# Two steps' scores in one phase around each output product, in a kernel of two attentions

## The chip, the cores and the metric

The kernel runs on one core of a Trainium2 chip. The metric is the time of one execution on the device in microseconds; a kernel's time is the median over its runs. The profile is taken from one further execution. TensorE (PE, with its weight loads PEld) multiplies, VectorE (DVE) and ScalarE (ACT) read the results from eight accumulation banks of 128 partitions by 512 numbers, GpSimd (POOL) works in the local memory only, and SP issues most transfers.

## What is computed

Two attention layers with 32 heads of 18 columns over 2048 positions, each with its own input, projections and output weights; their outputs stand side by side.

```python
# A: each position looks at 8 positions, 2 apart
logits = einsum("bhsd,bhswd->bhsw", q, kg) * scale      # masked before position 0
o = einsum("bhsw,bhswd->bhsd", softmax(logits), vg)
a = o.reshape(B, S, D) @ A_wo
# B: each position looks at all positions
scores = einsum("bhqd,bhkd->bhqk", q, k) * scale
o = einsum("bhqk,bhkd->bhqd", softmax(scores), v)
b = o.reshape(B, S, D) @ B_wo
return concatenate([a, b], axis=-1)                      # (1, 2048, 1152)
```

All is in 32-bit numbers. A projection or output product is split into high and low parts, so that one product of 128 by 288 is 27 or 30 matrix multiplications ("pieces") of at most 64 rows each.

## The kernel before

After a stage of projections (lines 373 to 725) the kernel runs 512 steps (the loop at line 1165). Heads are taken in 8 groups of 4, queries in 4 blocks of 512, keys in 16 tiles of 128; `g`, `b` and `kt` name a step's group, block and tile. A step has these parts on TensorE, in the order in which the program lists them, which is the order in which the engine takes them:

- Four score multiplications of 56 rows by 512 columns (`score`, line 269), two on each half of the array's rows (`r` is the half); the halves work side by side. ACT turns each result into exponentials `e` (line 276). `e` tiles come from two pools, six and two of them, by a count modulo 8.
- Three banks of maxima (`maximum` and `parts_of_maximum`, line 158): for a later block the scores are computed a first time, and DVE takes the largest of each 256 numbers (line 166), so that the exponentials don't overflow. One of the three banks is made of two quarters, one from each row half; since two row halves must not write one bank at once, an empty instruction on ACT (line 249) stands between them as a link of semaphores (`sync`).
- The values: four multiplications of all 128 rows by 19 columns (`weigh`, line 739), each recorded as two, which add the previous step's exponentials times the values into the bank `po` over 16 steps. The array has to change from row halves to full height and back once a step.

The banks: scores have four in turn, maxima three ("else"), `po` one.

Beside the steps runs an agenda: functions with due steps (`later`, `plan`, `due`), which issue the loads, the POOL and DVE work of the first attention and the closing of a block. Among them are the output products. Those of the first attention (`finished`, `sums_of_a`; 32 halves) and some of the second (`quarter` by way of `half`) are put into the list `inside`, and the next step takes one before its fourth score (line 1180). `beside` (line 1044) then computes the product in two chains, each row half into a bank of its own, piece by piece in turn, and puts two more maxima between them. ACT copies one bank to `y` (line 973), DVE adds the other (line 974). So a step with a product has five banks of maxima, and the next step three.

When a block's last tile is weighed, `finish` copies `po` (line 749 on ACT, line 752 on DVE). When the maxima have all been taken, near the end, two steps' values are done together (`paired`, line 1195), and products wait in the list `waiting`.

Of the kernel before, what the change touches and what calls it, by code (L numbers as in the profile page):

```python
# [23 lines left out]
NT = S // 128  # L24
NB = S // 512
SCALE = DH ** -0.5
# [7 lines left out]
ALL = NG * STEPS  # L34
# [25 lines left out]
def two_attentions(ctx: ExitStack, tc, xa, wa, woa, xb, wb, wob, out):  # L60
# [5 lines left out]
    nc = tc.nc  # L66
# [39 lines left out]
    step = 0  # L106

    def later(n, f):
        agenda[step + n].append(f)
# [5 lines left out]
    def due():  # L115
        for f in agenda.pop(step, []):
            f()
# [96 lines left out]
    given = [0, 0]  # L214
# [44 lines left out]
    e_room = None  # L259
    counted = [-1]  # L260

    def score(g, b, kt, h, kind="scores", between=None):

        assert (g, b) in placed
        qs, ks = sets[g % 3]
        p, r = divmod(h, 2)
        ps = bank(kind)
        at = slice(64 * r, 64 * r + 56)
        nc.tensor.matmul(ps, ks[at, p, 128 * kt : 128 * kt + 128], qs[at, b, p], start=True, stop=True)  # L269
        if between:  # L270
            between()

        counted[0] += 1
        early = counted[0] % 8 < 6
        e = (e_room if early else work).tile([128, 512], F32, name="e", bufs=6 if early else 2)
        nc.scalar.activation(e, ps, AF.Exp, scale=SCALE)  # L276
        return e

    vs = {}

# [92 lines left out]
    every = slice(0, 512)  # L373
# [4 lines left out]
    with (tc.tile_pool(name="x", bufs=1, side="right") as xp,  # L378
# [4 lines left out]
        early = ExitStack()  # L383
# [98 lines left out]
        if True:  # L482
# [9 lines left out]
            chunks = [[(0, 0, 128)], [(0, 128, third - 128), (D, 0, 256 - third)], [(D, 256 - third, 128)]]  # L492
# [24 lines left out]
            for c in range(5):  # L517
                one, other = (load, nc.scalar.dma_start) if c % 2 == 0 else (nc.scalar.dma_start, load)
# [9 lines left out]
            x = [t[0] for t in xs]  # L528
# [69 lines left out]
            for t in range(NT):  # L598
                ps = bank()
# [78 lines left out]
            for k in range(2, 14):  # L678
                n = 46 if k == 2 else 36 + 4 * k
# [14 lines left out]
            for t in order[:4]:  # L694
                ps = bank()
# [18 lines left out]
            for c, b in order:  # L714
                n = min(128, 3 * D - 128 * c)
# [3 lines left out]
            es = []  # L719
# [10 lines left out]
        step = 0  # L730
# [5 lines left out]
    def weigh(*steps):  # L736
        for g, b, kt, es in steps:
            for i in range(4):
                nc.tensor.matmul(po[32 * i : 32 * i + 19], vs[g][:, kt, 19 * i : 19 * i + 19], es[i],  # L739
                                 start=kt == 0, stop=kt == NT - 1)  # L740
        if kt == NT - 1:
            finish(g, b)
# [116 lines left out]
    def local(j):  # L859

        st = {}
# [98 lines left out]
            x.append(last)  # L960

        def finished(h, n):
            inside.append(lambda: sums_of_a(h, n))

        def sums_of_a(h, n):
            his, los = zip(*wo["a"])
            w = his[:4], los[:4], his[4], los[4]
            cols = slice(288 * h, 288 * h + 288)
            if h == 0:
                st["y"] = ys["a", j, n] = work.tile([128, D], F32, name="y", bufs=4)  # L970
            one, two = beside("scores", *(halves(r, 0, w, st["x", n], cols, slice(0, 128), True) for r in range(2)))
            y = st["y"][:, cols]
            nc.scalar.activation(y, two, AF.Copy)
            behind_scores.append(lambda: nc.vector.tensor_add(y, one, y))

# [50 lines left out]
    ys = {}  # L1026
# [13 lines left out]
    inside = []  # L1040
# [3 lines left out]
    def beside(kind, *both):  # L1044

        sums_ = [bank(k)[:, :288] for k in (kind, None)]
        turns = [[(sums_[r], *ab, i == 0, i == len(t) - 1) for i, ab in enumerate(t)] for r, t in enumerate(both)]
        pair = kind and sum(given) + 2 <= NG * NB * PIECES * 2
        if pair:

            for r in range(2):
                turns[r].insert(6 + 4 * r, None)
        for i in range(max(map(len, turns))):
            for r in range(2):
                if i < len(turns[r]):
                    if turns[r][i]:
                        ps, a, b, start, stop = turns[r][i]
                        nc.tensor.matmul(ps, a, b, start=start, stop=stop)  # L1058
                    else:
                        maximum(r)()  # L1060
        if pair:

            rings["else"].append(rings["else"].pop(0))
        return sums_

    def sum_of(y, t, h, chunks, kind=None):

        pos, cols = slice(128 * t, 128 * t + 128), slice(288 * h, 288 * h + 288)
        both = []
        for r in range(2):  # L1070
            both.append([])
            for c, (hi, lo) in enumerate(chunks):
                at = slice(64 * r, min(64 * r + 64, hi.shape[0]))
                whi, wlo = wo["b"][c]
                both[r] += [(a[at, pos], w[at, cols]) for a, w in ((hi, whi), (hi, wlo), (lo, whi))]
        one, two = beside(kind, *both)
        if kind:
            nc.vector.tensor_copy(y, one)
        else:
            nc.scalar.activation(y, one, AF.Copy)  # L1080
        nc.vector.tensor_add(y, two, y)
# [27 lines left out]
    def full(b, new):  # L1109
        def half(t, h):  # L1110
            if total - sum(given) > 4:
                inside.append(lambda: quarter(t, h, "scores"))
            else:
                waiting.append(lambda: quarter(t, h))

        def quarter(t, h, *kind):
            if h == 0:
                ys[t, b] = work.tile([128, D], F32, name="y", bufs=4)
            sum_of(ys[t, b][:, 288 * h : 288 * h + 288], t, h, [*olds[b], new], *kind)
            if h == 1:  # L1120
                later(1, lambda: load(out[512 * b + 128 * t : 512 * b + 128 * t + 128, D:], ys[t, b]))

        return [(4 + 2 * t + h, lambda t=t, h=h: half(t, h)) for t in range(4) for h in range(2)]

# [34 lines left out]

    total = early + rest  # L1160

    paired = False
    due()
    step += 1
    while step < ALL:
        n, kt = divmod(step, NT)
        g, b = divmod(n, NB)
        es = [None] * 4

        whole = total - sum(given) > 1  # L1170
        parts = (bool(begun) or total - sum(given) > 3) and step not in copied

        ps = bank() if inside and whole else None


        ahead = kt == 0 and (n < 6 or n >= 24)
        part = [parts_of_maximum()] if parts and not ahead else []
        for h in (0, 2, 1, 3):

            if inside and h == 3:  # L1180
                inside.pop(0)()
# [52 lines left out]
```

## Time and profile before

| | |
|---|---|
| runs | 1604.53 us median of 3 (1604.03 to 1605.91) |
| profiled execution | span 1603.8 us from its first to its last instruction; what lies around it is not in the trace |
| TensorE clock granted | 0.998 |
| PE busy | 1590.0 us, 99% |
| DVE busy | 1383.7 us, 86% |
| ACT busy | 1217.7 us, 76% |
| POOL busy | 960.1 us, 60% |

PE's ends are modelled and its instructions overlap, so its 99% does not say that nothing could be gained there. The steps fill the time from about 423 us to the end; before that, and in the last 100 us, other limits hold, so the prices of a step are read from the timeline of that stretch. In a row of the timeline stand the start, the length, engine, line, operation, result and inputs; rows that belong together are merged, and x5 says how many there are. A bracket gives how long the engine stood idle before, and what ended it.

### The profile page before, as it was taken

The numbers are of one execution on the slowest core, as the hardware profiler recorded it, in microseconds if no ns is written. First come the engines' busy times: TensorE is split into PE (matmuls) and PEld (weight loads), VectorE is DVE, ScalarE is ACT, GpSimd is POOL, SyncE is SP. The second block draws the span as 40 slices with busy tenths as digits, with TensorE's granted clock in tenths as the row PEclk, the third lists the DMA queues.
The fourth block names the chain that finished last, engine by engine and source line by source line (L and its number), as shares of the span: only waits on it lengthen the run. The fifth ranks groups of instructions, "written<-read, shape, count | busy, mean of one in ns | idle before, by whom it ended". The sixth has DMA issues, their size and how long they took to land.

```text
span 1603.8 us, 35232 instructions
## 1 busy us (share of the span) xinstructions
PE 1590.0 (99%) x13388; PEld 950.3 (59%) x13388; DVE 1383.7 (86%) x2347; ACT 1217.7 (76%) x2438; POOL 960.1 (60%) x792
## 2 busy tenths in 40 slices
PE   9999999999999999999999999999999999999998
PEld 7999888999543444444444444444444444445676
DVE  5299899999999999999999999999999999999512
ACT  6423441221699999999999999999999999898655
POOL 2405742201166995896797897797797797772100
PEclk9999999999999999999999999999999999999999
DMA  8937954522312362254326325422632231144111
GB/s 247 235 125 199 258 173 124 162 92 80 74 37 67 72 143 72 59 133 99 73 76 143 74 78 131 105 78 61 135 100 65 65 96 32 50 163 157 62 39 60
DMA packets 186058, 172.11 MB, mean 107 GB/s; under 512 B 119152, under 2 KB 132976, under 8 KB 184160
## 3 DMA queue, kind: packets, MB, share of 16 engines
q1 hardware_dynamic: 181024, 158.31, 36.1%
q0 software_dynamic: 4032, 10.63, 3.1%
q8 instruction: 105, 1.72, 0.5%
q10 hardware_dynamic: 832, 0.92, 0.2%
q14 instruction: 65, 0.53, 0.1%
HBM read 96.94 MB, written 71.90 MB: 105 GB/s over the span
## 4 chain that ended last, share of the span: by engine, by line
PE 91%; DVE 4%; DMA 2%; ACT 2%; issue 0%; POOL 0%; SPq 0%; POOLq 0%; DVEq 0%; ACTq 0%
PE po L739 29%; PE bank L269 18%; PE bank L158 17%; PE bank L361 15%; PE bank L1058 8%; PE bank L298 5%; DVE mx L166 3%; ACT e L276 1%; DMA dqk<-olo 1%; DMA dqk<-ohi 1%; DMA den<-o 0%; POOL xlo L409 0%; PE bank L513 0%; DVE as L900 0%; ACT lg L909 0%
## 5 line engine op out<-in xcount | busy, mean ns | idle before, releaser
L166 DVE TENSOR_REDUCE mx<-bank 128x2 f32<-128x512 f32 x2048 | 1288.3, 684 | 110.5 <-PE bank L158 82.6
L276 ACT ACTIVATE e<-bank 128x512 f32<-128x512 f32 x2048 | 1049.9, 608 | 46.6 <-PE bank L269 43.3
L158 PE MATMUL bank<-ks,qs 54*128 54x256 f32 (+1 forms) x2530 | 787.7, 378 | 4.2 <-DVE mx L166 2.5
L158 PEld LDWEIGHTS bank<-ks,qs 54*128 54x128 f32 x2530 | 408.8, 184 | 445.7 <-DVE mx L166 397.0
L269 PE MATMUL bank<-qs,ks 56*128 56x512 f32 x2048 | 568.9, 426 | 0.0
L739 PE MATMUL po<-e,v 128*19 128x512 f32 x4096 | 537.7, 599 | 0.0
L269 PEld LDWEIGHTS bank<-qs,ks 56*128 56x128 f32 x2048 | 299.7, 184 | 29.3 <-ACT e L276 25.2
L882 POOL TENSOR_TENSOR pr<-aq,akv 128x1024 f32<-128x1024 f32 x72 | 158.3, 2200 | 15.8 <-DMA akv<-da 13.0
L925 POOL TENSOR_TENSOR pr<-lg,akv 128x1024 f32<-128x1024 f32 x72 | 158.3, 2199 | 0.6
L886 POOL TENSOR_TENSOR pr<-pr 128x1024 f32<-128x1024 f32 x64 | 152.6, 2384 | 5.0
L739 PEld LDWEIGHTS po<-e,v 128*19 128x19 f32 x4096 | 70.5, 97 | 129.1 <-issue 123.6
L689 ACT ACTIVATE ohi<-bank 128x512 f32<-128x512 f32 (+1 forms) x56 | 30.4, 595 | 150.8 <-issue 104.2
L361 PE MATMUL bank<-xhi,ahi 64*128 64x512 f32 (+1 forms) x448 | 114.3, 387 | 0.0
L361 PE MATMUL bank<-xhi,alo 64*128 64x512 f32 (+1 forms) x448 | 109.6, 387 | 0.0
L361 PE MATMUL bank<-xlo,ahi 64*128 64x512 f32 (+1 forms) x448 | 105.8, 388 | 0.1
L926 POOL TENSOR_TENSOR pr<-pr 128x512 f32<-128x512 f32 x72 | 92.4, 1284 | 5.6
L409 POOL TENSOR_TENSOR alo<-raw,ahi 128x512 fp32r<-128x512 f32 (+1 forms) x14 | 17.6, 1255 | 121.4 <-ACT ahi L408 113.2
L501 POOL TENSOR_TENSOR olo<-olo,ohi 128x512 fp32r<-128x512 f32 x36 | 46.2, 1294 | 70.9 <-ACT ohi L500 62.8
L101 POOL CAST mh<-mt 128x32 fp32r<-128x32 f32 x32 | 6.7, 210 | 101.5 <-DVE mt L183 96.3
L361 PEld LDWEIGHTS bank<-xhi,ahi 64*128 64x128 f32 (+1 forms) x448 | 64.1, 182 | 4.4
L499 ACT ACTIVATE olo<-bank 128x512 f32<-128x512 f32 x36 | 21.2, 589 | 56.4 <-PE bank L361 31.4
L361 PEld LDWEIGHTS bank<-xhi,alo 64*128 64x128 f32 (+1 forms) x448 | 60.2, 182 | 4.4
(203 smaller groups left out, 1846.2 us busy)
## 6 DMA issues: line engine op xcount, KB each, us to landing
do<-n SPq DMA_DIRECT2D x28, 512.0 KB
da<-ohi SPq DMA_DIRECT2D x52, 256.0 KB
akv<-da SPq DMA_DIRECT2D x64, 175.5 KB
out<-y SPq DMA_DIRECT2D x32, 288.0 KB
qs<-dqk SPq DMA_DIRECT2D x30, 288.0 KB
ks<-dqk SPq DMA_DIRECT2D x30, 288.0 KB
at<-dao SPq DMA_DIRECT2D x60, 128.0 KB
rec<-drec SPq DMA_DIRECT2D x29, 256.0 KB
```

The lines of the kernel that those rows point to most:

```text
L158: return nc.tensor.matmul(ps if part is None else ps[:, 256 * r : 256 * r + 256], qs[at, b, p, 128 * t : 128 * t + 128], ks[at, p, 512 * k ...
L166: nc.vector.tensor_reduce(at, ps.rearrange("q (s n) -> q s n", s=2), axis=AX.X, op=ALU.max)
L269: nc.tensor.matmul(ps, ks[at, p, 128 * kt : 128 * kt + 128], qs[at, b, p], start=True, stop=True)
L276: nc.scalar.activation(e, ps, AF.Exp, scale=SCALE)
L298: nc.tensor.matmul(ps, a, b, start=c == i == 0, stop=c == 4 and i == 1)
L361: nc.tensor.matmul(ps, a, b, start=start, stop=stop)
L739: nc.tensor.matmul(po[32 * i : 32 * i + 19], vs[g][:, kt, 19 * i : 19 * i + 19], es[i], start=kt == 0, stop=kt == NT - 1)
L882: nc.gpsimd.tensor_mul(pr, ap(st["q"][:, 2 * c], (SUB, 2), (0, W), (1, SUB)), window(st["k"], c))
L886: nc.gpsimd.tensor_add(st["pr"], st["pr"], pr)
L925: nc.gpsimd.tensor_mul(at, ap(st["lg"], (0, 2), (SUB, W), (1, SUB)), window(st["v"], c))
L926: nc.gpsimd.tensor_add(at[:, :, :4], at[:, :, :4], at[:, :, 4:])
L1058: nc.tensor.matmul(ps, a, b, start=start, stop=stop)
```

## The change

A new function `together` does two steps at once when a product is in `inside`, the tile is not the first of its block, one step is waiting to be weighed, at least 8 maxima are left, and it is not the very end. It takes one of the four score banks for the product alone. In a first half of the phase the product's pieces of row half 0 run as one chain into that bank, and between them, on row half 1, four scores (two for each of the two steps) and four maxima, each a full bank. Then an empty instruction on ACT links to the second half: the pieces of row half 1 go on in the same bank, beside four scores and four maxima on row half 0. The order is made by sorting with a spacing of 133 for pieces and 235 for the others. An exponential is issued to ACT one score later than before. At the end ACT copies the one bank to `y`; DVE's addition is gone. Then the values of the waiting step and of the first of the two are done in one go, 8 multiplications.

`sums_of_a` and `quarter` return the pairs of operands instead of computing when they are called so. `e` tiles are six and six, by a count modulo 12; the space for the four more comes from halving the scratch for the transfers that POOL issues.

```diff
-    def score(g, b, kt, h, kind="scores", between=None):
+    def score(g, b, kt, h, kind="scores", between=None, put_off=False):
...
-        counted[0] += 1
-        early = counted[0] % 8 < 6
-        e = (e_room if early else work).tile([128, 512], F32, name="e", bufs=6 if early else 2)
-        nc.scalar.activation(e, ps, AF.Exp, scale=SCALE)
-        return e
+        def exponential():
+            counted[0] += 1
+            early = counted[0] % 12 < 6
+            e = (e_room if early else work).tile([128, 512], F32, name="e", bufs=6)
+            nc.scalar.activation(e, ps, AF.Exp, scale=SCALE)
+            return e
+        return exponential if put_off else exponential()
...
+            both = [halves(r, 0, w, st["x", n], cols, slice(0, 128), True) for r in range(2)]
+            if not alone:
+                return both, y
...
+    def together(both, y):
+        at = [(*divmod(s // NT, NB), s % NT) for s in (step, step + 1)]
+        es = [[None] * 4 for _ in range(2)]
+        ps = bank("scores")[:, : y.shape[1]]
+        held = rings["scores"].pop()
+        exps = deque()
+        def one(i, h):
+            f = score(*at[i], h, put_off=True)
+            exps.append(lambda: es[i].__setitem__(h, f()))
+        def others(r):
+            return [f for i in range(2) for h in (r, r + 2) for f in (lambda i=i, h=h: one(i, h), lambda: maximum(r)())]
+        def piece(r, k):
+            a, b = both[r][k]
+            return nc.tensor.matmul(ps, a, b, start=r == k == 0, stop=r == 1 and k == len(both[1]) - 1)
+        def in_turn(*lanes):
+            for _, f in sorted(((at + every * k, f) for fs, at, every in lanes for k, f in enumerate(fs)), key=lambda p: p[0]):
+                f()
+                while len(exps) > 1:
+                    exps.popleft()()
+        last = []
+        in_turn(([lambda k=k: last.append(piece(0, k)) for k in range(len(both[0]))], 0, 133), (others(1), 1, 235))
+        between = nc.scalar.nop()
+        sync(between, last[-1])
+        in_turn(([lambda k=k: sync(piece(1, k), between) if k == 0 else piece(1, k) for k in range(len(both[1]))], 240, 133),
+                (others(0), 0, 235))
+        while exps:
+            exps.popleft()()
+        nc.scalar.activation(y, ps, AF.Copy)
+        rings["scores"].append(held)
+        return [(*at[i], es[i]) for i in range(2)]
...
+        if inside and kt and len(ready) == 1 and total - sum(given) >= 8 and step + 4 < ALL:
+            new = together(*inside.pop(0)(False))
+            due()
+            step += 1
+            weigh(*ready, new[0])
+            ready[:] = new[1:]
+            due()
+            step += 1
+            continue
...
-    nc = bacc.Bacc("TRN2", target_bir_lowering=False, num_devices=1)
+    nc = bacc.Bacc("TRN2", target_bir_lowering=False, num_devices=1, dynamic_dma_scratch_size=8192)
```

More of the change, by code (lines that the diff above doesn't have):

```diff
@@ L962, in finished, with sums_of_a @@
         def finished(h, n):
-            inside.append(lambda: sums_of_a(h, n))
-        def sums_of_a(h, n):
+            inside.append(lambda alone: sums_of_a(h, n, alone))
+        def sums_of_a(h, n, alone):
             his, los = zip(*wo["a"])
@@ L970, in sums_of_a @@
                 st["y"] = ys["a", j, n] = work.tile([128, D], F32, name="y", bufs=4)
-            one, two = beside("scores", *(halves(r, 0, w, st["x", n], cols, slice(0, 128), True) for r in range(2)))
             y = st["y"][:, cols]
+            both = [halves(r, 0, w, st["x", n], cols, slice(0, 128), True) for r in range(2)]
+            if not alone:
+                return both, y
+            one, two = beside("scores", *both)
             nc.scalar.activation(y, two, AF.Copy)
@@ L1064, in beside, with sum_of @@
         return sums_
-    def sum_of(y, t, h, chunks, kind=None):
+    def sum_of(y, t, h, chunks, kind=None, alone=True):
         pos, cols = slice(128 * t, 128 * t + 128), slice(288 * h, 288 * h + 288)
@@ L1075, in sum_of @@
                 both[r] += [(a[at, pos], w[at, cols]) for a, w in ((hi, whi), (hi, wlo), (lo, whi))]
+        if not alone:
+            return both, y
         one, two = beside(kind, *both)
@@ L1111, in half @@
             if total - sum(given) > 4:
-                inside.append(lambda: quarter(t, h, "scores"))
+                inside.append(lambda alone: quarter(t, h, "scores", alone))
             else:
@@ L1118, in quarter @@
                 ys[t, b] = work.tile([128, D], F32, name="y", bufs=4)
-            sum_of(ys[t, b][:, 288 * h : 288 * h + 288], t, h, [*olds[b], new], *kind)
             if h == 1:
                 later(1, lambda: load(out[512 * b + 128 * t : 512 * b + 128 * t + 128, D:], ys[t, b]))
+            return sum_of(ys[t, b][:, 288 * h : 288 * h + 288], t, h, [*olds[b], new], *kind)
         return [(4 + 2 * t + h, lambda t=t, h=h: half(t, h)) for t in range(4) for h in range(2)]
@@ L1180, in two_attentions @@
             if inside and h == 3:
-                inside.pop(0)()
+                inside.pop(0)(True)
             es[h] = score(g, b, kt, h, between=(lambda: part.append(parts_of_maximum())) if parts and ahead and h == 0 else None)
```

## The prediction

> **What bounds the kernel now.** I read the page's header, its chain, one 100 us stretch of the steady part, and the list of waits, in this order.
>
> ```profile
> span 1603.8 us, 35232 instructions
> PE 1590.0 (99%) x13388; PEld 950.3 (59%) x13388; DVE 1383.7 (86%) x2347; ACT 1217.7 (76%) x2438; POOL 960.1 (60%) x792
> PE 91%; DVE 4%; DMA 2%; ACT 2%; issue 0%; POOL 0%; SPq 0%; POOLq 0%; DVEq 0%; ACTq 0%
> ...
> 1200.00:1300.00 100.00, 99.84 (x831) 46.60 (x825) 93.19 (x162) 94.07 (x187) 77.63 (x61) 1.00 0.22 56
> ...
> PEld bank L158 <- DVE mx L166: 397.0, 466, 1.6
> PEld po L739 <- issue: 123.6, 504, 0.3
> ```
>
> The stretch gives, after the time, the busy shares of PE, PEld, DVE, ACT and POOL. PE carries the chain, but DVE and ACT run at 93 and 94% beside it: work taken from PE is a gain only as far as those two can follow. The two waits come once a step, at its two turns: 504 times 0.25 us when the array goes from row halves (scores, maxima, products) to the full-height values, and 466 times on the way back, where PE loads a maximum's weights and the wait named is a maximum bank that DVE still reads. Now one product step and the step behind it, on TensorE, then on DVE:
>
> ```profile
> 603.07 0.38 PE L158 MATMUL bank<-ks,qs 54*128 54x256 f32 x1
> ...
> 605.54 0.31 PE L1058 MATMUL bank<-wolo,at 64*128 64x288 f32 x2
> 605.67 0.31 PE L1058 MATMUL bank<-wohi,ahl 64*128 64x288 f32 x2
> 605.80 0.29 PE L1058 MATMUL bank<-wolo,ahl 64*128 64x288 f32 x1
> 605.82 0.40 PE L269 MATMUL bank<-qs,ks 56*128 56x512 f32 x1
> 605.93 0.39 PE L158 MATMUL bank<-ks,qs 54*128 54x512 f32 x1
> 606.25 1.05 PE L739 MATMUL po<-e,v 128*19 128x512 f32 x8
> 607.23 0.38 PE L158 MATMUL bank<-ks,qs 54*128 54x256 f32 x1
> 607.24 0.50 PE L269 MATMUL bank<-qs,ks 56*128 56x512 f32 x1
> 607.46 0.40 PE L158 MATMUL bank<-ks,qs 54*128 54x512 f32 x1
> 607.57 0.52 PE L269 MATMUL bank<-qs,ks 56*128 56x512 f32 x2
> 607.81 0.29 PE L158 MATMUL bank<-ks,qs 54*128 54x256 f32 x1
> 607.93 0.39 PE L269 MATMUL bank<-qs,ks 56*128 56x512 f32 x1
> 607.94 0.39 PE L158 MATMUL bank<-ks,qs 54*128 54x512 f32 x1
> 608.27 1.05 PE L739 MATMUL po<-e,v 128*19 128x512 f32 x8
> 609.25 0.39 PE L158 MATMUL bank<-ks,qs 54*128 54x256 f32 x1
> ```
>
> ```profile
> 603.72 3.32 DVE L166 TENSOR_REDUCE mx<-bank 128x2 f32<-128x512 f32 x5
> 606.96 0.45 DVE L974 TENSOR_TENSOR y<-bank,y 128x288 f32<-128x288 f32 x1
> 607.89 3.31 DVE L166 TENSOR_REDUCE mx<-bank 128x2 f32<-128x512 f32 x5 [0.48 <-PE bank L158]
> ```
>
> The step with the product runs 603.07 to 607.23: 3.18 us in row halves and 0.98 of values; the next one 1.04 and 0.98. The pair takes 6.18. There are 32 such pairs; the last one:
>
> ```profile
> 1472.58 0.18 PEld L158 LDWEIGHTS bank<-ks,qs 54*128 54x128 f32 x1 [0.85 <-DVE mx L166]
> ...
> 1478.69 0.18 PEld L158 LDWEIGHTS bank<-ks,qs 54*128 54x128 f32 x1 [0.85 <-DVE mx L166]
> ```
>
> It takes 6.11. I set 6.15 for all, the middle of the two.
>
> **The unit prices.** On one row half, a 512-column score or maximum takes 0.235 us (607.46 to 607.93 on half 1 is two of them); a 288-column product piece 0.13 (605.54, 605.67, 605.80); the first of a phase 0.10 more (607.24 to 607.57 is 0.33); from the last piece to the values 0.08 (605.93 plus 0.235 to 606.25). A maximum begun at 607.46 is taken up by an idle DVE at 607.89: 0.43 later. What DVE needs, and when PE gets a bank back, shows where the stream of projections waits for it:
>
> ```profile
> 88.61 1.88 DVE L166 TENSOR_REDUCE mx<-bank 128x2 f32<-128x512 f32 x3
> ```
> ```profile
> 89.34 0.18 PEld L158 LDWEIGHTS bank<-ks,qs 54*128 54x128 f32 x1 [0.27 <-DVE mx L166]
> ...
> 89.94 0.18 PEld L158 LDWEIGHTS bank<-ks,qs 54*128 54x128 f32 x1
> ```
> ```profile
> L166 DVE TENSOR_REDUCE mx<-bank 128x2 f32<-128x512 f32 x2048 | 1288.3, 684 | 110.5 <-PE bank L158 82.6
> L276 ACT ACTIVATE e<-bank 128x512 f32<-128x512 f32 x2048 | 1049.9, 608 | 46.6 <-PE bank L269 43.3
> ```
>
> One reduction lasts 0.68, the next starts 0.60 behind it (1.88 less 0.68, halved). They end at 89.29 and 89.89, and PE loads at 89.34 and 89.94: 0.05 later. So a bank whose reduction starts at R can be filled again at R + 0.73, and a maximum that waits paces everything behind it in PE's order at 0.60.
>
> **The change part by part.** In the changed program's order of instructions 34 joint phases stand: the 32 products of the first attention and 2 of the second; other steps keep their order. The pair's matmul work is the same: 8 scores, 8 maxima (before 5 and 3), one product, 16 value matmuls. Three things are saved. (1) Values of both steps in one go, which the end of the kernel already does:
>
> ```profile
> 1541.55 1.91 PE L739 MATMUL po<-e,v 128*19 128x512 f32 x16
> 1543.40 0.40 PE L1058 MATMUL bank<-qs,qs 64*128 64x288 f32 x2
> ```
>
> That is 1.85 against 0.98 + 0.98: 0.11 less. (2) One turn into row halves and out: the 0.10 and the 0.08. (3) On DVE the addition at 606.96, 0.45, since both halves end in one bank; ACT's copy of it (0.41) stays.
>
> PE alone: phase one, product on half 0 (0.10 + 14 x 0.13 = 1.92) beside four scores and four maxima on half 1 (0.10 + 8 x 0.235 = 1.98). Phase two begins on half 0 at 1.92 with a score; the product's first piece on half 1 waits for ACT's empty instruction, which waits for the last piece of phase one (begun at 1.79 and 0.29 long, like the row at 605.80, plus two hops of 0.05, as from 89.29 to 89.34 above): about 2.2. Thirteen pieces more bring it to 3.9, the turn to 4.0. With the values 5.85: 0.30 less than 6.15, and 34 times that is 10 us. Behind that waiting piece stand, in PE's order, all later scores and maxima of the phase, so its wait is also theirs.
>
> But there are three banks for eight maxima. The k-th maximum (from 0) is begun by PE at 0.335 + 0.47k in phase one; DVE takes the first at 0.335 + 0.43 = 0.77 and the k-th at 0.77 + 0.60k. The maximum k + 3 needs that bank: at 0.77 + 0.60k + 0.73. Number 3 may start at 1.50 (PE comes at 1.75: no wait), number 4 at 2.10 (2.2: none), number 5 at 2.70 (2.67), number 6 at 3.30 (3.17), number 7 at 3.90 (3.77). From the fifth on DVE paces PE. Number 7 ends at 3.90 + 0.235 + 0.10 for the restart, with two product pieces behind it in the order (3.90 + 0.10 + 0.26); plus 0.08: the phase lasts 4.33, the pair 6.18. So of the 0.30, 0.33 goes back into a new wait of PE on DVE inside the phase, and while the 1.85 of values run, DVE empties its last banks by 0.77 + 7 x 0.60 + 0.68 = 5.65 and idles to 6.18 + 0.77. What is late next after the removed turn is thus DVE, and the saved addition does not help it, as it stood behind the last reduction.
>
> Bounds: without restart penalties 4.22, pair 6.07, minus 0.08. Upwards: one in eight pairs has the block's closing reduction in the chain (0.28, a mean of 0.035), and a DVE operation of the first attention may stand in front: 0.1 together, 6.28, plus 0.13. I take 6.20, near the worked 6.18, as the closing reductions are certain: 0.05 x 34 = 1.7 us more.
>
> ```profile
> L176 DVE TENSOR_REDUCE m<-mx 128x16 f32<-128x128 f32 x23 | 6.3, 276 | 0.0
> ```
>
> The smaller edits I set at nothing. Twelve e tiles for eight: the row of e above waits for a bank from PE, never for its tile. The halved scratch concerns the transfers that POOL issues, all before 310 us; POOL stood idle before them for 5.4 us in three places, and as much again would fit into the 40% of the span in which POOL does nothing.
>
> ```profile
> L140 POOL DMA_DIRECT2D ks<-dqk x18: 571/603/1297, 56.7 to 307.8; - x18
> ...
>   DMA qs<-dqk: 5.4, 3
> ```
>
> Agenda work (SP loads, POOL pieces) of the first step of a pair is issued up to 4 us later; out stores and operand loads have several steps in hand. At the end two products of the second attention move behind the last maximum, at the same streaming price; one turn fewer, about 0.2, against more banks to empty there: zero, with 1 us to either side.
>
> Two rules of the Trainium skill bear on this, on the page TensorEngine Tiling (Array Packing). Under Key Properties it says that a change of tiling mode drains the array; the 504 waits above agree, and by this rule alone the change gains the 10 us of the first rival. Under PSUM Bottleneck it says that tiling speeds the matmuls but not the emptying of the banks; the pace of 0.60 at 89.34 and 89.94 agrees, and by that rule the gain is not there. The rows decide for the second.
>
> **The rivals.** *Faster*: PE sets the pair (5.85): 1594. For it: PE's 91% of the chain, and DVE idle 0.48 at 607.89. Against it: DVE would have to do eight reductions at 0.47 each. *Slower*: the wait on ACT's empty instruction. ACT works in order, and where a block has just ended it has a copy of the values in front:
>
> ```profile
> 656.82 0.38 PE L158 MATMUL bank<-ks,qs 54*128 54x256 f32 x1
> ```
> ```profile
> 657.22 0.63 ACT L749 ACTIVATE o<-po 128x512 f32<-128x512 f32 x1
> 657.69 1.63 ACT L276 ACTIVATE e<-bank 128x512 f32<-128x512 f32 x3
> ```
>
> The step there began at 656.82; the third exponential behind that copy starts 0.51 after the second (1.63 less 0.61, halved), at about 1.9 of the step, and the empty instruction passes once its product is done at 2.1. If it had to wait for one more exponential, 0.51, the product's second half would begin at 2.7 and, with 0.10 for the restart, end at 4.5, the phase at 4.6, the pair at 6.45: 0.30 x 34 = 10 us, 1615. It decides from a delay of about 0.25 on (2.2 + 0.10 + 13 x 0.13 + 0.08 = 4.07 without one), where the thirteen pieces pass DVE's 4.33. Against it: the put-off exponential stands behind the empty instruction.
>
> **How the numbers follow.** The profiled execution has a span of 1603.8; the median of the runs is 1604.53, 0.7 above, and I add the difference to the median: 1604.5 + 1.7 = 1606. DVE as the new pacer: 0.75, its own range 1602 (34 x -0.08) to 1609 (34 x 0.13). PE-bound: 0.10, 1594. ACT's wait: 0.15, 1615 at full size, less where only some phases have it. The range 1600 to 1613 leaves out most of the first rival and the upper half of the second. This kernel's measurement can tell about 0.2%, 3.2 us: same covers 1601.3 to 1607.7. Of the 0.75, 0.10 lies below it, 0.42 in it, 0.23 above. Faster 0.20, same 0.42, slower 0.38.
>
> **What would show it.** Joint phases of about 4.3 us and values of 1.85; inside them PE's weight loads for maxima waiting on DVE from the fifth or sixth on; DVE with its eight reductions 0.60 apart in a row, then idle for about a microsecond until the step behind. If phases of 4.0 appear, banks were not the limit and the forecast is too high by up to 10 us. If a long wait of a product piece on ACT's sequencer shows in the middle, the second rival holds. If steps without a product change from the 2.02 us of 607.23 to 609.25, something that I set at nothing wasn't.

## The result and the profile after

The changed kernel takes 1608.87 us (median of 6 runs, 1608.71 to 1610.13) against 1603.82 us (median of 6, 1602.59 to 1605.91) for the kernel before on the same chip: a ratio of 1.003, 95% interval 1.0019 to 1.0042. It is slower by 5 us, 0.3%.

The page of the changed kernel, header and engines, then its list of waits (total us, times, longest):

```profile
span 1607.0 us, 35002 instructions
PE 1592.5 (99%) x13320; PEld 971.7 (60%) x13320; DVE 1362.0 (85%) x2311; ACT 1214.3 (76%) x2440; POOL 959.7 (60%) x792
```
```profile
PEld bank L158 <- DVE mx L166: 339.6, 403, 2.1
PEld po L742 <- issue: 133.1, 538, 0.3
...
PEld bank L269 <- ACT e L277: 24.7, 51, 0.8
PEld bank L1187 <- ACT e L277: 23.8, 28, 0.8
```

DVE's busy time falls by 22 us and TensorE (PE) has fewer weight loads held up by DVE (403 for 466), and yet the span is longer: what was removed was not what set the time. (The second line counts more waits than before, 538 for 504, though there are fewer turns: in a pair's 16 values the weight loads pause twice more, 0.31 each at 605.11 and 605.54, while the multiplications go on.) Where the time lies shows best by stretches. Each row gives the stretch, its length and the busy time of PE, PEld, DVE, ACT and POOL, then the clock, the DMA share and GB/s; the stretches run from the first product of the first attention to the step of the first product of the second, and from there to the end. Before:

```profile
603.07:1487.40 884.33, 882.31 (x7294) 411.15 (x7290) 826.09 (x1417) 836.27 (x1655) 690.58 (x527) 1.00 0.36 93
1487.40:1603.80 116.40, 110.42 (x1246) 82.02 (x1242) 35.01 (x76) 63.37 (x135) 5.88 (x12) 0.99 0.13 50
```

After:

```profile
600.30:1489.24 888.94, 886.19 (x7231) 427.90 (x7227) 806.95 (x1385) 832.61 (x1655) 690.38 (x527) 1.00 0.36 92
1489.24:1607.00 117.76, 111.01 (x1242) 83.08 (x1238) 33.07 (x72) 63.89 (x137) 5.90 (x12) 0.99 0.14 52
```

The stretch with the 32 products is 4.61 us longer, the tail 1.36. The start, up to the first product, is 2.77 shorter, but 1.8 of that belong to the one execution that was profiled before: wherever a run has both figures, its time is 1.7 to 1.9 us above its span, so the span of 1603.8 stands for a time of about 1605.6, which is 1.8 above the median, while the profiled execution after took 1608.85, as the median. One joint phase of the changed kernel, the first, in the timeline, on DVE and then on PE:

```profile
601.07 4.88 DVE L166 TENSOR_REDUCE mx<-bank 128x2 f32<-128x512 f32 x8
607.16 3.90 DVE L166 TENSOR_REDUCE mx<-bank 128x2 f32<-128x512 f32 x6 [1.22 <-PE bank L158]
```
```profile
600.30 0.40 PE L1187 MATMUL bank<-wohi,at 64*128 64x288 f32 x1
...
602.58 0.40 PE L1187 MATMUL bank<-wohi,at 64*128 64x288 f32 x1
...
603.01 0.50 PE L158 MATMUL bank<-ks,qs 54*128 54x512 f32 x1
...
603.61 0.49 PE L158 MATMUL bank<-ks,qs 54*128 54x512 f32 x1
...
604.21 0.50 PE L158 MATMUL bank<-ks,qs 54*128 54x512 f32 x1
604.21 0.40 PE L1187 MATMUL bank<-wolo,at 64*128 64x288 f32 x1
604.45 0.29 PE L1187 MATMUL bank<-wohi,ahl 64*128 64x288 f32 x1
604.67 1.91 PE L742 MATMUL po<-e,v 128*19 128x512 f32 x16
606.51 0.38 PE L158 MATMUL bank<-ks,qs 54*128 54x256 f32 x1
...
607.54 1.05 PE L742 MATMUL po<-e,v 128*19 128x512 f32 x8
608.53 0.38 PE L158 MATMUL bank<-ks,qs 54*128 54x256 f32 x1
...
609.24 0.50 PE L269 MATMUL bank<-qs,ks 56*128 56x512 f32 x1
609.24 0.49 PE L158 MATMUL bank<-ks,qs 54*128 54x512 f32 x1
609.67 1.05 PE L742 MATMUL po<-e,v 128*19 128x512 f32 x8
```

DVE runs eight reductions in a row, 0.60 apart ((4.88 less 0.68) by seven), then stands idle for 1.22. The last three maxima start 0.60 apart too, 2.71, 3.31 and 3.91 after the phase began, and the last two pieces of the product queue behind the very last. The row-half part takes 4.37, the values 1.84, the pair 6.21.

This is one of ten such phases. Before the exponentials of the other 22 a block's closing copy stands on ACT, as in the next one, which begins at 618.79:

```profile
619.21 0.63 ACT L752 ACTIVATE o<-po 128x512 f32<-128x512 f32 x1
619.69 4.16 ACT L277 ACTIVATE e<-bank 128x512 f32<-128x512 f32 x8
```
```profile
620.38 0.18 PEld L269 LDWEIGHTS bank<-qs,ks 56*128 56x128 f32 x1
...
621.26 0.18 PEld L1187 LDWEIGHTS bank<-wohi,at 64*128 64x128 f32 x1
...
622.77 0.44 PE L158 MATMUL bank<-ks,qs 54*128 54x512 f32 x1
```

The first exponential is late, so the fourth score finds its bank late (620.38). The product's second half, its pieces on row half 1 behind the link, begins at 621.26, which is 2.47 into the phase; in the ten it begins at 2.28. The last maximum starts at 3.98 instead of 3.91. The row-half part takes 4.39, nearly the same, but it is made up in another way: until the second half begins and from there on it takes 2.28 + 2.10 in the ten, 2.47 + 1.92 in the 22 (medians).

Over all 32 the part takes 4.40 on average and the pair 6.24, against 6.154 before: 0.087 more each, 2.8 us in all. The rest of the 4.61 lies behind the pair: there the first step's row halves take 1.03 (606.51 to 607.54) and the second's 1.14 (608.53 to 609.67). In the kernel before the two steps behind a pair have 1.07 and 1.03 (medians of all): 0.064 less, some 28 times, 1.8 us.

### The profile page after: what moved, and what is told of

Same layout as the page of the kernel before. It is cut to its first block, busy times and chain, and to the rows that moved or that the text cites. A ratio compares the mean times of both kernels' runs of the same rounds, so it can differ in the third digit from the quotient of the medians.

```text
span 1607.0 us, 35002 instructions
## 1 busy us (share of the span) xinstructions
PE 1592.5 (99%) x13320; PEld 971.7 (60%) x13320; DVE 1362.0 (85%) x2311; ACT 1214.3 (76%) x2440; POOL 959.7 (60%) x792
## 4 chain that ended last, share of the span: by engine, by line
PE 91%; DVE 4%; ACT 2%; DMA 1%; issue 1%; POOL 0%; SPq 0%; DVEq 0%; POOLq 0%; ACTq 0%
PE po L742 29%; PE bank L269 18%; PE bank L158 17%; PE bank L364 15%; PE bank L301 5%; PE bank L1187 4%; PE bank L1064 4%; DVE mx L166 3%; ACT e L277 1%; DMA den<-o 0%; DMA raw<-xa 0%; POOL xlo L412 0%; DMA first<-xb 0%; SPq L509 0%; DMA dqk<-ohi 0%
## 5 line engine op out<-in xcount | busy, mean ns | idle before, releaser
L158 PE MATMUL bank<-ks,qs 54*128 54x512 f32 (+1 forms) x2462 | 791.2, 382 | 4.3 <-DVE mx L166 3.1
L158 PEld LDWEIGHTS bank<-ks,qs 54*128 54x128 f32 x2462 | 403.3, 184 | 386.8 <-DVE mx L166 339.6
L269 PE MATMUL bank<-qs,ks 56*128 56x512 f32 x2048 | 608.8, 428 | 0.1
L742 PE MATMUL po<-e,v 128*19 128x512 f32 x4096 | 531.2, 598 | 0.0
L269 PEld LDWEIGHTS bank<-qs,ks 56*128 56x128 f32 x2048 | 309.2, 184 | 35.2 <-ACT e L277 24.7
L1187 PE MATMUL bank<-wohi,at 64*128 64x288 f32 x480 | 103.2, 304 | 0.0
L1187 PEld LDWEIGHTS bank<-wohi,at 64*128 64x128 f32 x480 | 74.5, 184 | 27.3 <-ACT e L277 23.8
L1187 PE MATMUL bank<-wolo,at 64*128 64x288 f32 x240 | 73.2, 305 | 0.0
```

The costliest lines, as they stand in the source:

```text
L158: return nc.tensor.matmul(ps if part is None else ps[:, 256 * r : 256 * r + 256], qs[at, b, p, 128 * t : 128 * t + 128], ks[at, p, 512 * k ...
L1187: return nc.tensor.matmul(ps, a, b, start=r == k == 0, stop=r == 1 and k == len(both[1]) - 1)
```

## The experiments

Times beside an experiment are medians with their range, ratios are to the kernel before on the same chip. "Phase" is the row-half part of a joint step pair, averaged over the 32 products of the first attention.

**The edits set at nothing.** The kernel before, with the twelve e tiles and the halved scratch alone:

```diff
-        early = counted[0] % 8 < 6
-        e = (...).tile([128, 512], F32, name="e", bufs=6 if early else 2)
+        early = counted[0] % 12 < 6
+        e = (...).tile([128, 512], F32, name="e", bufs=6)
...
+ dynamic_dma_scratch_size=8192
```

> The kernel before with twelve e tiles in place of eight and the halved scratch for POOL's transfers, nothing else. Theory 1 (the loss lies in the joint phases and the steps behind them): no change, 1603.8 within 1.5 us, steps without a product 2.02 to 2.05 us. Rival (the new places of tiles, or fewer descriptors for POOL, cost something by themselves): 1607 to 1609, with the loss spread over all steps or over the first 420 us.

1603.11 us (1602.69 to 1604.89), ratio 0.9997 (0.9987 to 1.0007), steps of the same lengths as before. These edits cost nothing, and gain at most 2 us. In this trace too the first product comes early, at 600.24; in the traces of the runs below it lies between 599.3 and 602.1, so an execution can be ahead or behind there by some 3 us.

**DVE out of the way.** In joint phases the reductions read the first 128 of each 256 numbers, so half of the numbers are left out there:

```diff
-            nc.vector.tensor_reduce(at, ps.rearrange("q (s n) -> q s n", s=2), ...)
+            nc.vector.tensor_reduce(at, ps.rearrange("q (s n) -> q s n", s=2)[:, :, : 128 if short[0] else 256], ...)
```

> The changed kernel, but in the joint phases each reduction reads only the first 128 of each 256 numbers, so those maxima are not the true ones. Theory 1 (DVE paces the phase through its three banks): the reductions of a phase come 0.35 to 0.45 us apart in place of 0.60, no maximum waits for a bank, the phase falls from 4.38 to 4.05 us, and the kernel by 34 x 0.33 = 11 us, to 1598. Rival (TensorE itself needs 4.38, by turns, by the chain in one bank or by the link between the halves): the phase stays at 4.3 to 4.4, 1608 to 1609.

1607.23 us (1606.49 to 1609.44), ratio 1.002 (1.0011 to 1.003): a miss. Two kinds of phases appear. Ten take 4.19 on average; the 22 in which a block's closing copy stands on ACT in front of the exponentials take 4.39, for 4.41 before the edit. On ACT, in one of the 22 (it began at 618.58):

```profile
618.99 0.63 ACT L754 ACTIVATE o<-po 128x512 f32<-128x512 f32 x1
619.46 4.13 ACT L279 ACTIVATE e<-bank 128x512 f32<-128x512 f32 x8
```

The first exponential starts 0.88 into the phase instead of about 0.5, and ACT has eight of them, 0.5 apart, before it. So DVE sets the ten phases, and its relief takes 0.19 off them, all of it in the second half (1.91 for 2.10). The 22 keep both their halves, 2.46 and 1.92: DVE's pace is not what they wait for. Something else holds the ten at 4.19.

**The other order of score and maximum**, the maximum first in both halves, so that DVE starts earlier:

```diff
-            return [f for i in range(2) for h in (r, r + 2) for f in (lambda i=i, h=h: one(i, h), lambda: maximum(r)())]
+            ... for f in (lambda: maximum(r)(), lambda i=i, h=h: one(i, h))]
```

> The changed kernel with maximum before score in each pair of the joint phase, in place of score before maximum. Theory 1: the first reduction starts 0.33 us earlier (at 0.43 of the phase in place of 0.77), and with it the whole chain; maximum 7 can begin at 3.56 in place of 3.90, the score behind it ends at about 3.9, the phase falls from 4.38 to between 4.1 and 4.2, the kernel by 34 x 0.18 to 0.28 = 6 to 10 us, to 1599 to 1603. Rival (TensorE's own work or turns set the phase): no change, 1608 to 1609.

1610.38 us (1608.47 to 1611.51), ratio 1.0041 (1.0026 to 1.0056), phase 4.42. In a phase that began at 618.15 the last maximum starts 3.67 after it, 0.31 earlier than in the changed kernel's phase at this place (622.77). But then a score stands behind it, which begins at 4.01 and lasts until the values at 4.40. DVE's pace is the same, only what follows it in PE's order changed; the expectation let that score end at about 3.9, which leaves time for one of the two.

**The step behind the pair.** Where does its 0.064 come from? In the changed kernel the first exponential behind the pair starts at 607.12, 0.61 after the step's first load (607.77 less 607.23 is 0.54 in the kernel before). The rows of line 277 between 607.0 and 607.2 (durations in ns):

```profile
L277 ACTq EVENT_SEMAPHORE  x1: 17/17/17, 607.1 to 607.1; - x1
L277 ACT ACTIVATE e<-bank x1: 600/600/600, 607.1 to 607.1; 128x512 f32<-128x512 f32 x1
```

An instruction for a further wait stands in front of that exponential. The Trainium skill says of this, under Identifying Dependency Chains on its page Perfetto Trace Analysis, that instructions which wait for several engines may get such semaphore instructions ahead of them; the trace agrees, and shows what it costs here, 0.07. ACT then runs exponentials without a pause through both steps, the fourth score of the second step finds its bank a little late, and the restart lengthens it (0.50 and 0.49 at 609.24, for 0.44 and 0.42 at this place in the kernel before). The experiment puts the bank that the product had held back at another place of the ring of score banks:

```diff
-        rings["scores"].append(held)
+        rings["scores"].append(rings["scores"].pop(0))
+        rings["scores"].insert(2, held)
```

> The changed kernel with another order of the four score banks behind a joint phase: first those of the last two exponentials, then the product's, then the one used longest ago. By that the first exponential behind the phase has one wait in the program in place of two. In the changed kernel it starts 0.60 us behind the start of its step, before the change 0.53, and the second step behind a pair lasts 1.14 us in row halves in place of 1.03, in 28 places. Theory (the second wait makes ACT 0.07 late, the fourth score of the second step finds its bank 0.02 late, and the array's restart costs 0.10): first exponential at 0.53, second step 1.03, the kernel down by 28 x 0.11 = 3 us, to 1606. Rival (the exponential is late because ACT stood idle for 1.65 us, or the second step is long for another reason): still 0.60 and 1.14, 1608 to 1609.

1607.76 us (1606.95 to 1609.57), ratio 1.0027 (1.0018 to 1.0037). The first exponential starts at 0.54 again (medians; 0.60 in the changed kernel). The second step is back at 1.07, the first stays at 1.03, the phases at 4.39: 28 times 0.071 are 2.0 us in the trace, where 3 was expected. The whole time cannot tell it: the ratio to the kernel before, 1.0027 for 1.003, lies within both intervals. The semaphore instruction stands in front of a later exponential now, where it passes while another one runs. The cause of the second step's loss is shown.

**Starting DVE earlier without the late score.** Maximum first on row half 1, score first on row half 0:

```diff
+                    for f in (lambda i=i, h=h: one(i, h), lambda: maximum(r)())[:: -1 if r else 1]]
```

> The changed kernel with the maximum before the score on row half 1 (first half of the phase) and the score before the maximum on row half 0 (second half), so that the phase begins and ends with a maximum. Theory, revised by the two runs before (DVE paces the phase through three banks; with DVE out of the way ACT paces it through three score banks; in the run with all maxima first the last maximum came 0.23 earlier, but a score stood behind it): the first reduction starts at 0.54 as there, the last maximum can begin at 0.54 + 4 x 0.60 + 0.73 = 3.67, which is where TensorE comes to it anyway, and nothing is behind it but product pieces. The phase falls from 4.38 to between 4.05 and 4.2, the kernel by 34 x 0.18 to 0.33 = 6 to 11 us, to 1598 to 1603. Rival (the phase's length is TensorE's own, by the chain in one bank and the link between the halves): 4.35 to 4.40, 1608 to 1610.

> The same with the other order of the score banks behind a joint phase (one wait in place of two on the next exponential). Theory: 2 us less than without it (28 x 0.07), the second step behind a pair 1.07 in place of 1.14, 1596 to 1601, faster than the kernel before. Rival: the second step stays at 1.14 and the time that of the run without it.

The mixed order alone: 1606.89 us (1602.78 to 1608.24), ratio 1.0019 (1.0009 to 1.0028), phase 4.28. With the ring of the experiment before: 1604.82 us (1602.19 to 1605.86), ratio 1.0001 (0.9992 to 1.0011), phase 4.26, the second step behind it 1.07. The loss is gone, without a gain: the phases again part into ten of 4.19 and 22, behind a copy, of 4.29. In this order the second half of the 22 begins on time, 2.28 by the median, and lasts 2.00; what holds it there no run separates. In the third experiment of this kind the products of the second attention stay outside joint phases as well:

```diff
-        if inside and kt and len(ready) == 1 ...
+        if inside and not second and kt and len(ready) == 1 ...
```

> The same again, with the two products of the second attention outside the joint phases, as before the change. Theory (the tail behind the products of the first attention became 1.4 us longer because two products wait for the maxima's end and then stand three in a row in one step): the stretch from the first of the second attention's products to the end falls by 1.4 us, to 1595 to 1600. Rival (the tail is longer for another reason, such as the order of its last steps): no change against the run before it.

1604.06 us (1601.64 to 1606.33), ratio 1.0001 (0.9992 to 1.0011). No difference in the comparison; in the trace the tail, from the step of the second attention's first product on, is 1.0 us shorter than in the changed kernel. Up to the start of the last step it is 105.08 long, as before the change (105.12; changed kernel 106.55). Behind it 0.4 come on top, 11.70 for 11.27 and 11.24: the last copy on DVE waits 1.35 for a store of `y` in place of 0.68. Of all traces only this one and that of the last experiment show it.

**Both engines relieved.** Beside the short reductions, only two of four exponentials are taken in joint phases and their e tiles used twice; half of the exponentials of these phases are left out:

```diff
-            exps.append(lambda: es[i].__setitem__(h, f()))
+            exps.append(lambda: es[i].__setitem__(h, f() if h < 2 else es[i][h - 2]))
```

> The changed kernel, whose joint phases take 4.40 us, relieved of both engines: in joint phases the reductions read the first 128 of each 256 numbers, and only two scores of each step's four get an exponential (the other two values are multiplied with the same e tiles). Both parts leave out computation. Theory (DVE paces the phase through three banks of maxima, and ACT, uncovered when DVE is relieved, through three banks of scores): with both out of the way TensorE sets the phase at the 4.0 us that the first rival of the prediction worked out; 4.40 - 4.0 = 0.4 us, 32 times: 13 us less than the changed kernel, about 1596. Rival (the empty instruction in the middle, or the order of TensorE's own work, holds the phase): phases stay at 4.18 to 4.36 as with the short reductions alone, about 1604 to 1607.

1605.98 us (1604.76 to 1607.67), ratio 1.0013 (1.0004 to 1.0022): the theory missed by 10 us, and for the ten phases without a copy the rival holds: they still take 4.18. In the first of them (from 600.95) weights load for the product's second half at 603.22 and for the values at 605.12:

```profile
602.64 0.18 PEld L1189 LDWEIGHTS bank<-wolo,ahl 64*128 64x128 f32 x1
...
603.22 0.18 PEld L1189 LDWEIGHTS bank<-wohi,at 64*128 64x128 f32 x1
...
604.77 0.18 PEld L1189 LDWEIGHTS bank<-wohi,ahl 64*128 64x128 f32 x1
605.12 0.14 PEld L744 LDWEIGHTS po<-e,v 128*19 128x19 f32 x8 [0.16 <-issue]
```

The product's own chain fills the phase: 2.27 for the first half and the link through ACT's empty instruction, 1.90 for the second, 4.17 together, with nothing else in the way. That is the floor of this form of the phase as long as its halves follow each other directly. And a phase behind a block's copy (from 619.23):

```profile
619.65 0.63 ACT L754 ACTIVATE o<-po 128x512 f32<-128x512 f32 x1
620.12 1.17 ACT L279 ACTIVATE e<-bank 128x512 f32<-128x512 f32 x2
```
```profile
620.82 0.18 PEld L271 LDWEIGHTS bank<-qs,ks 56*128 56x128 f32 x1
620.82 0.18 PEld L1189 LDWEIGHTS bank<-wolo,at 64*128 64x128 f32 x1
...
621.69 0.18 PEld L1189 LDWEIGHTS bank<-wohi,at 64*128 64x128 f32 x1 [0.17 <-ACTq L1201]
```

The fourth score has no bank until the first exponential, late behind the copy, has read it (620.77, 620.82). The product's chain stands behind that score in PE's order, pays for the wait and for the restart, and its second half starts 2.46 into the phase instead of 2.27, as in the changed kernel (2.47). So it is the copy, not the number of exponentials, that makes these phases 0.2 longer: they keep 4.38 with half of them.

**ACT relieved alone**, the same edit on the changed kernel with whole reductions:

> The changed kernel with two exponentials for each step's four in joint phases (two of four e tiles are used twice, so half of the exponentials of these phases are left out); the reductions are whole. Theory (DVE's reductions, 0.60 apart, set the phase at 4.38; ACT's pace lies below it): phases stay at 4.33 to 4.40, time 1607 to 1609. Rival (ACT is already part of what sets the phase, through the exponentials behind a block's closing copy or the empty instruction in the middle): phases fall below 4.3, time below 1606.

1608.13 us (1607.16 to 1610.02), ratio 1.0029 (1.0018 to 1.004); phase 4.39 behind a copy and 4.37 without. DVE in the first:

```profile
601.49 4.87 DVE L166 TENSOR_REDUCE mx<-bank 128x2 f32<-128x512 f32 x8
```

The same eight reductions in the same time. The number of ACT's exponentials sets no phase. The copy itself stays in this run, so it does not show that ACT has no part. The row-half part until the product's second half begins, and from there on (medians):

| | 10 without a copy | 22 behind a copy |
|---|---|---|
| changed kernel | 2.28 + 2.10 | 2.47 + 1.92 |
| DVE relieved | 2.28 + 1.91 | 2.46 + 1.92 |
| half of the exponentials | 2.28 + 2.10 | 2.46 + 1.93 |
| both | 2.27 + 1.90 | 2.46 + 1.92 |

In the ten, DVE makes the second half 0.19 longer. In the 22 the copy makes the first half 0.19 longer, and the second half is already at its floor, whether DVE is relieved or not. That they come to 4.38 and 4.39 is a coincidence. Without the copy DVE would presumably hold the 22 as it holds the ten; no run takes away the copy alone.

**The values of both steps apart.** The waiting step's values move to the middle of the phase:

```diff
         between = nc.scalar.nop()
         sync(between, last[-1])
+        weigh(ready.pop(0))
...
-            weigh(*ready, new[0])
+            weigh(new[0])
```

> The changed kernel with the waiting step's values moved from behind the joint phase to its middle, between the two row halves: the values of both steps together are undone, and the product's chain and the banks stay. Theory (the bank wait paces the phase): while TensorE does 0.98 us of values in the middle, DVE empties its banks, so the second half starts at about 3.2 us with free banks and needs 2.0 as TensorE alone would; 3.2 + 2.1 + 0.98 = 6.3 for the pair against 6.24 now, so that what was saved by doing the values together was nearly all paid back in the wait: 1608 to 1611. Rival (the turns count in full and the wait stays where it is): 6.24 + 0.13 for the values + 0.25 for the turn = 6.6 for the pair, 32 times 0.38: 1620.

1608.4 us (1607.39 to 1612.78), ratio 1.004 (1.0026 to 1.0054); the pair takes 6.23 on average, as with the values together (6.24). On DVE:

```profile
600.05 2.48 DVE L166 TENSOR_REDUCE mx<-bank 128x2 f32<-128x512 f32 x4
603.08 2.48 DVE L166 TENSOR_REDUCE mx<-bank 128x2 f32<-128x512 f32 x4 [0.55 <-PE bank L1187]
```

While the values run, DVE empties its banks and waits for the next maximum. On average the removed turn, the centre of the change, is worth nothing here. The average hides two cases: without a copy the pair is 0.13 shorter with the turn put back (6.09 for 6.22), behind a copy 0.04 longer (6.29 for 6.25). Without a copy each half takes 2.06, 4.12 together, less than the 4.18 with both engines relieved: the values in the middle give DVE time and also cover the link through ACT's empty instruction.

**The copy earlier too.** The mixed order, the ring, no joint phases for the second attention, and a joint phase begins only from the third step of a block on:

```diff
-        if inside and not second and kt and len(ready) == 1 ...
+        if inside and not second and kt > 1 and len(ready) == 1 ...
...
-            if inside and h == 3:
+            if inside and h == 3 and kt != 1:
```

> The mixed order with the score banks' ring mended and the second attention's products outside joint phases (measured equal to the kernel before), and in addition a joint phase begins only from the third step of a block on, so that the block's closing copy on ACT lies a step earlier. Nothing is left out. Theory (behind that copy ACT paces the phase through the score banks, 4.28 on average against 4.18 where there is no copy): all phases at 4.18 to 4.22, 23 times 0.1: 2.3 us less, about 1601.7, ratio 0.998 to 0.999 to the kernel before. Rival (the copy is not what lengthens those phases): phases stay at 4.28, time 1604.

1602.14 us (1601.12 to 1605.21), ratio 0.9993 (0.9983 to 1.0002). 27 of the 32 phases are below 4.25 now, the other five between 4.33 and 4.66 (mean 4.23, median 4.20, 2.28 + 1.92), which shows the copy's share. By stretches, as above:

```profile
600.53:1482.64 882.11, 879.72 (x7231) 426.59 (x7228) 805.68 (x1385) 830.42 (x1655) 690.45 (x527) 1.00 0.35 93
1482.64:1599.42 116.78, 110.40 (x1246) 82.01 (x1242) 35.01 (x76) 63.37 (x135) 5.89 (x12) 0.99 0.14 54
```

The first is 2.2 us shorter than in the kernel before, the tail 0.4 longer, behind the last step. That is the most that this form gave; the interval still holds no difference.

## Why the prediction was right

The forecast was 1606.0 with 1602 to 1609 for its likeliest case, DVE as the new pacer; 1608.87 was measured. The direction was right, and in ten of the 32 phases the mechanism; in the other 22 it was another one that happens to give the same length. The kernel before lay at 1603.82 in these runs, so the change costs 5.05 where 1.7 was forecast, more than the 4.4 (34 x 0.13) at which that case's own range ends. That the time still lies below 1609 is luck: the kernel before ran 0.7 faster than the median from which the sum started. Three terms of the sum were too small. In the two profiles they make 2.8 + 1.8 + 1.4 = 6.0; the medians show 1.0 less, which no run tells from noise. The prediction's "0.7 above" compares the span of one execution with the median of others; what lies around a span is 1.8 here. It changes no term of the sum.

- **DVE paces the phase: right, in place and size, for ten phases of 32.** The maxima 5, 6 and 7 were forecast at 2.70, 3.30 and 3.90 and stand at 2.71, 3.31 and 3.91; eight reductions 0.60 apart, then idle; with DVE relieved these phases fall from 4.38 to 4.19. In the 22 behind a copy the maxima stand at 2.91, 3.49 and 3.98 (medians), and relieving DVE changes nothing (4.39). The rule of the Trainium skill that spoke against the change (TensorEngine Tiling (Array Packing), PSUM Bottleneck: tiling speeds the matmuls, not the emptying of banks) fits both kinds: in the ten DVE empties its banks 0.60 apart, in the 22 a score bank is emptied late by ACT and costs 0.19.
- **The phase at 4.33, the pair at 6.18, 6.20 with the additions: 0.04 low.** The first phase takes 4.37, the mean 4.40, the pair 6.24. By the 32 pairs that is 2.8 us for the 1.7 of the sum. That the mean comes so near is partly luck: the copy's 0.19 happens to equal DVE's.
- **"Other steps keep their order", and so their time: wrong.** The prediction named the test, a step without a product that changes, and it did: the two steps behind a pair take 0.064 more. The order is the same, but not the waits in front of one exponential. About 1.8 us; in the trace the experiment on the ring gave the time back.
- **The tail at zero, with 1 us to either side: it cost 1.4.** With the second attention's products outside joint phases all of it goes in the trace of the steps, and 0.4 come back behind the last step, as a wait for a store.
- **Tiles and scratch at nothing: right** (0.9997, 0.9987 to 1.0007).
- **The faster rival, PE alone at 4.0 and 5.85: too low.** With both engines relieved the ten phases without a copy take 4.18 and the pair 6.02. The second half starts at 2.27, where 2.2 stood, and the sum of 4.0 left out the restart that the other rival's sum, 4.07, has. So without DVE's pace and without the copy the change could have gained about 0.13 a pair, 4.5 us, not 10. The Trainium skill says that a change of mode drains the array (same page, Key Properties); the turn is there in the trace (0.25 of idle weight loads at 607.54), but its removal gained nothing: the pair takes 6.24 without it and 6.23 with it.
- **The slower rival, ACT in front of the product's second half: at work in 22 of the 32 phases, by another path and at another price.** No long wait on the empty instruction appears in the changed kernel. The copy frees a score bank late, the fourth score and the product's chain behind it stand, and the second half starts 0.19 later. The prediction let such a delay decide from 0.25 on, because its 4.07 for the chain alone was 0.11 too low (4.18): 0.19 is enough to reach 4.38. Removing only DVE's pace therefore gained little (1607.23); the mixed order with the copy a step earlier brought the phases to 4.20.

What stays open: what holds the second half at 2.00 behind a copy in the mixed order, and why the wait for the last store is longer where the second attention's products stay outside joint phases.

## What to carry to other kernels

When two steps are merged to save a turn of the array, count for each engine that empties banks how many results it has to take in the merged phase and how many banks they go through; the turn also gave those engines time to catch up. Where several limits lie close together (here 4.38 by DVE, 4.39 behind a copy on ACT and 4.18 by the product's chain), removing one shows the next, so relieve them one by one and all together before a gain is promised. Sort the phases by what stands in front of them and split them at a point in their middle: equal lengths had two causes here, and their mean hid both. And look at the first instructions behind a reordered phase: a wait more in front of one of them can move the steps that were not touched.

## What was not expected of the hardware

- A score that is held up by 0.02 us for its bank pays for a restart: the one at 609.24 starts 0.14 behind the matmul before it, in the kernel before 0.12, and it and the maximum beside it last 0.50 and 0.49, there 0.44 and 0.42, in an unbroken stream 0.39.
- One more semaphore instruction ahead of an idle ACT's first exponential delays it by 0.07 (0.61 for 0.54); in front of an exponential that waits behind another no cost shows.
- The link of two chains through ACT's empty instruction takes, from the weight load of the last piece to that of the next chain's first, 0.58 (602.64 to 603.22), where pieces follow each other at 0.13; scores and maxima run beside it, but the product's later pieces all wait for it, and they end the phase.
